# An instruction order ranked by the work behind each instruction, and weight splits taken off GpSimd

## The chip, the core and the metric

The kernel runs on one core of a Trainium2 chip. The metric is device time in microseconds (us) for one execution. A core has five instruction streams that run side by side and meet at semaphores: PE (TensorE, matrix products), DVE (VectorE), ACT (ScalarE), POOL (GpSimd) and SP (SyncE, which here only issues DMAs). Each stream runs its own instructions strictly in the order in which they were written into it, so an instruction that waits holds up everything behind it on its engine.

## What is computed

Three stages follow one another on 2304 tokens of width 512:

```
attention, 4 batches x 8 heads, 576 positions, head size 64, causal:
    scores = q k^T / 8 + cum[i] - cum[j],   cum = cumsum(log(clip(f)))
    x = softmax(scores) v                          -> 2304 x 512
first MLP:   h = x w_in  (512 x 2048);  g = h * tanh(softplus(h));  x = g w_out
second MLP:  h = x w2_in (512 x 1024);  s = h * softmax(h)
             out = (layernorm(s) * g_ln) w2_out
```

The four weight matrices arrive as 64-bit floats, q, k, v and f as 32-bit floats.

## The kernel before

**Products in three passes.** Every operand of a product is held as a high and a low half in f16, and a product is hi·hi + hi·lo + lo·hi, all accumulated in PSUM. A value therefore needs two element-wise passes before it can be used: one that makes the high half, one that makes the low half (value minus high half). The function `split` (L178) does this in one of three modes: mode 0 is one ACT pass for the high half and one DVE pass for the low half; mode 1 is an ACT pass that scales in place, a POOL pass for the high half and a POOL pass for the low half; mode 2 is two ACT passes and one POOL pass.

**Weights of the first MLP.** `w_in` and `w_out` are cut into eight tiles each of 128 x 1024 values (the class `Weight`, L95). A tile takes this way: `load` (L110) fetches 1 MB by DMA into one of two raw buffers that all sixteen tiles share; `conv` (L116) turns the 64-bit floats into 32-bit ones by three DVE passes (L123, L125, L127), after which the raw buffer is free for the next load; eight small matmuls (L146) form a Gram matrix that bounds the size of the values; after every two tiles, `bound` (L149) works out one power-of-two scale from it, by a chain of tiny DVE operations and one matmul across partitions; and `split` makes the two halves of both tiles. The sixteen tiles come in the order two of `w_in`, two of `w_out`, and so on (L684). Which mode each split takes is a string indexed by the tile number: `W1P = "00111111"` for `w_in` (tiles 0 and 1 in mode 0, tiles 2 to 7 in mode 1) and `W2P = "10"` for `w_out` (even tiles in mode 1, odd ones in mode 0), used at L602 and L609.

**Attention.** Per batch there are five query chunks of up to 128 rows. `step_s` makes scores on PE, `step_r` the maxima (DVE, L465) and exponentials (ACT, L467), `step_h` the halves (ACT, POOL or DVE for the high half, POOL at L506 for the low half), a DMA transpose (L511) turns them, `step_pv` multiplies by v (L537 to L539), and `fin` normalises, splits and transposes into `xT`, the input of the first MLP, which has three buffers of 256 tokens each.

**First MLP.** Nine blocks of 256 tokens. `up` (L764) makes h, `mish_a` to `mish_c` the activation and its halves (ACT, DVE, POOL at L791), `down` (L808) the second product. Block 0 takes each weight group as it becomes ready. **Second MLP.** The class `Stage2` (L1305), 18 tiles of 128 tokens: `first` (L1371 and the normalisation), a transpose through DMA, and `second` (L1411). Its weights are prepared as attention ends.

**The order of the work.** `emit` writes all instructions once, in an order set by hand-chosen leads. At the end `Order(tc).pin()` (L938) lays a new order over it. `Order.trace` rebuilds operations and dependencies, including the reuse of buffers in the order in which they were written; `weigh` gives each operation an estimated duration; `plan` (L1201) is a list scheduler that steps through time and, whenever an engine is free, starts the ready operation of lowest rank. It models a lock between DVE and POOL and one serial DMA resource. The rank of an operation is its number in the order written: `seq = self.plan([o.k for o in self.ops])` (L1297). The order found is then pinned on all five streams, so that it is what the chip executes. The estimated times decide only the order, not the times on the chip.

Of the kernel before, what the change touches and what calls it, by code (L numbers as in the profile page):

```python
# [51 lines left out]
HI0 = "a"  # L52
HI1 = "pd"
SP1 = "0000001"
W1P = "00111111"
W2P = "10"
QKV = "002"
W0C = 1
S2Q = 3
# [132 lines left out]
def emit(tc, q, k, v, f, w_in, w_out, w2_in, w2_out, g_ln, out):  # L192
# [404 lines left out]
    def w1_split(n):  # L597
        g, r = divmod(n, W1.group)
        if r == 0:
            W1.bound(g)  # L600
            nc.vector.tensor_copy(wps[g], W1.p(g))
        W1.split(n, on_pool=int(W1P[n % len(W1P)]))  # L602

    def w2_split(n):
        g, r = divmod(n, W2.group)
        if r == 0:
            W2.bound(g)
            nc.vector.tensor_tensor(rho[:, g:g + 1], wps[g], W2.p(g), op=ALU.mult)
        W2.split(n, on_pool=int(W2P[n % len(W2P)]))  # L609

# [340 lines left out]
ENGS = ("PE", "ACT", "POOL", "DVE", "SP")  # L951
ENG_OF = {"PE": "PE", "Activation": "ACT", "Pool": "POOL", "DVE": "DVE", "SP": "SP"}
EARLY = {"PE": 0.0, "ACT": 103.0, "DVE": 79.0, "POOL": 37.0, "SP": -45.0}
LATE = {"PE": 53.0, "ACT": 34.0, "DVE": 33.0, "POOL": 77.0, "SP": 27.0}
HEAD = 126.0
PERIOD = 3413.33
BACKLOG = 1500.0
LANDED = 600.0


def size_of(dt):
    s = str(dt)
    return 8 if "64" in s else 2 if "16" in s else 4
# [10 lines left out]
def on_chip(t):  # L974
    return type(t).__name__ == "Tile" and "DRAM" not in str(t._space)


class Order:
# [155 lines left out]
    def weigh_dma(self, o, i, acc):  # L1134
        out = next(b for t, b, w in acc if w)
        n = math.prod(c for _, c in list(out.ap)) * size_of(out.tensor.dtype)
        if type(i).__name__ == "InstDmaTransposeAnt":
            n //= 256
            o.d = {1536: 2000.0, 2048: 1860.0, 2560: 3050.0}.get(n, 1240.0)
            o.span = {512: 985.0, 1280: 2390.0, 1536: 2130.0, 2048: 2630.0, 2560: 3215.0}.get(n, 1410.0)  # L1140
            o.first = 1175.0
            return

        def run(b):
            r = 1
            for s, c in reversed(list(b.ap)[1 if on_chip(b.tensor) else 0:]):
                if c != 1 and s != r:
                    break
                r *= c
            return r * size_of(b.tensor.dtype)  # L1150

        rb = min(run(b) for t, b, w in acc)
        n //= rb
        o.d = {256: 590.0 if n >= 100 else 390.0, 4096: 368.0, 2048: 340.0}.get(rb, 500.0)
        o.span = n * rb / 300 if rb >= 1024 else n * (1.25 if n > 100 else 5.0) + 30
        o.first = 1020.0
# [44 lines left out]
    def plan(self, rank):  # L1201
# [24 lines left out]
        while todo:  # L1226
# [31 lines left out]
            elif e == "SP":  # L1258
                state["dma"] = max(state["dma"] - 20, t + o.first) + o.span
                end, seen = t + o.d, state["dma"] + LANDED  # L1260
                heapq.heappush(marks, state["dma"] - BACKLOG)
# [31 lines left out]
        self.end = state["end"]  # L1293
        return seq

    def pin(self):
        seq = self.plan([o.k for o in self.ops])  # L1297
        info = mybir.DependencyInfo(mybir.DependencyClass.NoSync, mybir.DependencyReason.DATA)
        for e in ENGS:
            row = [i for o in seq[e] for i, _ in o.ins]  # L1300
            for a, b in zip(row, row[1:]):
                self.tc.add_manual_dep(b, a.name, info, reason="order")
# [160 lines left out]
```

## Time and profile before

| | us |
|---|---|
| median of 3 runs (840.65 to 846.69) | 841.4 |
| the profiled execution | 845.53 |
| its span, first to last instruction | 843.7 |
| PE busy | 734.2 (87%) |
| DVE busy | 598.6 (71%) |
| ACT busy | 544.6 (65%) |
| POOL busy | 440.6 (52%) |

The span is 1.8 us shorter than the profiled execution, and that execution is 4.1 us above the median. The busy shares are averages over stages of different character: attention and weight preparation at the start, attention beside the first MLP in the middle, the second MLP at the end. The page cuts the span in 40 slices of 21.1 us each; a line of digits gives the busy share of an engine per slice in tenths.

### The profile page before, as it was taken

What the parts mean: (1) busy time and instruction counts of PE and PEld (TensorE: products, weight loads), DVE (VectorE), ACT (ScalarE), POOL (GpSimd) and SP (SyncE); (2) the same over time, 40 slices, a digit from 0 to 9 for tenths busy, and PEclk for the clock granted to TensorE, in tenths of its full rate; (3) what the DMA queues carried; (4) which work ended last, traced back from release to release, by engine and by line L of the source; (5) the groups of instructions that cost most, each with busy time, mean ns of one, the idle gap of its engine ahead of it and who ended that gap; (6) DMA issues with size and microseconds to landing.
All of it is one profiled execution on the core that took longest, in us unless ns stands there. A gap on an engine that the chain in (4) does not pass through costs nothing.

```text
span 843.7 us, 15751 instructions
## 1 busy us (share of the span) xinstructions
PE 734.2 (87%) x5822; PEld 456.5 (54%) x5822; DVE 598.6 (71%) x1158; ACT 544.6 (65%) x1201; POOL 440.6 (52%) x341
## 2 busy tenths in 40 slices
PE   0454245899999999899899999998999999999998
PEld 0333123556766666667566766675555554444443
DVE  5789979576976688867878963589978444656551
ACT  4743424898877998779878786788776554332331
POOL 2368377555678667776588783218357221213221
PEclk9999555999999999899999999999999999999999
DMA  9997694636699999997999743552224232355443
GB/s 226 207 206 213 210 220 97 122 58 129 137 169 163 190 159 182 174 187 147 195 169 163 146 80 76 163 199 77 63 56 87 63 71 63 88 97 115 103 88 85
DMA packets 328568, 114.83 MB, mean 136 GB/s; under 512 B 317676, under 2 KB 317676, under 8 KB 328492
## 3 DMA queue, kind: packets, MB, share of 16 engines
q1 hardware_dynamic: 328492, 113.84, 65.5%
q8 instruction: 45, 0.74, 0.4%
q14 instruction: 31, 0.25, 0.1%
HBM read 46.59 MB, written 9.55 MB: 67 GB/s over the span
## 4 chain that ended last, share of the span: by engine, by line
PE 53%; DVE 16%; ACT 10%; DMA 10%; issue 5%; POOL 5%; SPq 1%; POOLq 0%; DVEq 0%; ACTq 0%
PE x L808 14%; PE h L764 12%; PE h L1371 9%; PE o L1411 7%; PE pv L537 3%; DMA pT<-ph 2%; PE sp L418 2%; PE sp L419 2%; DMA rawk<-in_k_dram 2%; DMA w2i_r<-in_moe_w_in_dram 2%; POOL ph L506 1%; DMA rawv<-in_v_dram 1%; ACT p L467 1%; DVE wout L127 1%; POOL gt L791 1%
## 5 line engine op out<-in xcount | busy, mean ns | idle before, releaser
L808 PE MATMUL x<-wout,gt 128*128 128x512 f16 x864 | 213.9, 385 | 9.9 <-POOL gt L791 6.0
L764 PE MATMUL h<-xT,win 128*128 128x256 f16 x1728 | 209.9, 275 | 1.4 <-ACT th L777 1.4
L506 POOL TENSOR_TENSOR ph<-p,ph 128x512 f16<-128x512 f32 (+4 forms) x120 | 159.7, 1338 | 55.3 <-ACT ph L505 34.0
L764 PEld LDWEIGHTS <-win 128*128 128x128 f16 x1728 | 167.6, 99 | 35.1 <-issue 4.3
L791 POOL TENSOR_TENSOR gt<-th,gt 128x512 f16<-128x512 f32 x72 | 91.3, 1270 | 101.7 <-ACT gt L790 101.6
L808 PEld LDWEIGHTS <-gt 128*128 128x128 f16 x864 | 80.4, 99 | 90.3 <-POOL gt L791 10.0
L1399 POOL TENSOR_TENSOR z<-sl,z 128x1024 f16<-128x1024 f32 x18 | 39.2, 2178 | 140.4 <-DVE s2c L1378 87.8
L1371 PE MATMUL h<-w,x2T 128*128 128x512 f16 x432 | 96.0, 379 | 0.1
L1411 PE MATMUL o<-wo,zT 128*128 128x512 f16 x432 | 95.7, 379 | 0.1
L537 PE MATMUL pv<-vt,pT 128*128 128x64 f16 (+3 forms) x480 | 71.6, 202 | 12.7 <-DMA pT<-ph 12.6
L467 ACT ACTIVATE p<-sp,nm 64x64 f32<-64x64 f32 (+7 forms) x128 | 61.1, 483 | 33.1 <-DVE nm L465 16.8
L785 DVE SCALAR_TENSOR_TENSOR th<-ta,th 128x512 f32<-128x512 f32 x72 | 58.7, 817 | 23.4 <-ACT ta L784 20.4
L418 PE MATMUL sp<-ktr,qa 128*128 128x64 f16 (+6 forms) x304 | 58.6, 255 | 15.4 <-ACT p L467 13.1
L538 PE MATMUL pv<-vt,pT 128*128 128x64 f16 (+3 forms) x480 | 70.7, 197 | 0.0
L539 PE MATMUL pv<-vt,pT 128*128 128x64 f16 (+3 forms) x480 | 70.6, 197 | 0.0
L1411 PEld LDWEIGHTS <-zT 128*128 128x128 f16 x432 | 42.2, 98 | 51.3 <-DMA zT<-z 0.6
L1371 PEld LDWEIGHTS <-x2T 128*128 128x128 f16 x432 | 42.2, 98 | 50.6 <-DMA x2T<-x2d 0.6
L537 PEld LDWEIGHTS <-pT 128*128 128x128 f16 (+3 forms) x480 | 45.8, 102 | 42.5 <-issue 16.8
L419 PE MATMUL sp<-ktr,qb 67*128 67x64 f16 (+6 forms) x304 | 62.7, 256 | 4.2 <-DVE qb L383 3.7
L465 DVE TENSOR_REDUCE nm<-sp 128x1 f32<-128x320 f32 (+7 forms) x88 | 48.5, 562 | 22.4 <-PE sp L423 11.9
L1382 ACT ACTIVATE e<-h,s2c 128x1024 f32<-128x1024 f32 x18 | 21.7, 1204 | 64.2 <-DVE s2c L1380 64.2
L776 ACT ACTIVATE ta<-h,usc 128x512 f32<-128x512 f32 (+3 forms) x96 | 53.7, 576 | 14.3 <-PE h L764 14.2
(234 smaller groups left out, 1440.3 us busy)
## 6 DMA issues: line engine op xcount, KB each, us to landing
wi_r<-in_moe_w_in_dram SPq DMA_DIRECT2D x8, 1024.0 KB
wo_r<-in_moe_w_out_dram SPq DMA_DIRECT2D x8, 1024.0 KB
rawk<-in_k_dram SPq DMA_DIRECT2D x25, 256.0 KB
rawv<-in_v_dram SPq DMA_DIRECT2D x25, 256.0 KB
x2d<-x2h SPq DMA_DIRECT2D x18, 256.0 KB
out_dram<-ro SPq DMA_DIRECT2D x18, 256.0 KB
w2i_r<-in_moe_w_in_dram SPq DMA_DIRECT2D x4, 1024.0 KB
w2o_r<-in_moe_w_out_dram SPq DMA_DIRECT2D x4, 1024.0 KB
```

The costliest lines, as they stand in the source:

```text
L418: nc.tensor.matmul(d, qa[:, h, r0:r1_], k1, start=True, stop=False)
L419: nc.tensor.matmul(d, qb_[:67, h, r0:r1_], k2, start=False, stop=not diag)
L467: nc.scalar.activation(pv[:m, g * (i + 1) * P + off:g * (i + 1) * P + end], s3[:, g, off:end], AF.Exp, bias=nm[:m, g:g + 1], accum_out=rs[ ...
L506: nc.gpsimd.tensor_tensor(p4[:, :, 1], pv3, p4[:, :, 0], op=ALU.subtract)
L537: nc.tensor.matmul(o, pT[a0:a1, k, :m], vh, start=(c == 0), stop=False)
L538: nc.tensor.matmul(o, pT[a0:a1, k, :m], vl, start=False, stop=False)
L539: nc.tensor.matmul(o, pT[a0:a1, k + 1, :m], vh, start=False, stop=(c == i))
L764: nc.tensor.matmul(ph, win[:, (fi // 4) * NC1 + c, col:col + P], x[:, lx * NC1 + c, :], start=(m == 0), stop=(m == 3 * NC1 - 1))
L791: nc.gpsimd.tensor_tensor(gt[:, 1], th, gt[:, 0], op=ALU.subtract)
L808: nc.tensor.matmul(o, gt[:, lg, n % 2, t * P:(t + 1) * P], wout[:, fi, lw * 512:(lw + 1) * 512], start=(first and m == 0), stop=(last and ...
L1371: nc.tensor.matmul(h[:, half * 512:(half + 1) * 512], x[:, lx * NC1 + c, :], self.w2[:, half * NC1 + c, lw * 512:(lw + 1) * 512], start=(n ...
L1411: nc.tensor.matmul(o, zT[:, lz * NF2 + c, :], self.wo[:, c, lw * 512:(lw + 1) * 512], start=(n == 0), stop=(n == 3 * NF2 - 1))
```

## The change

Three things change. The mode strings `W1P` and `W2P` become `"0"`: all sixteen weight tiles of the first MLP are split in mode 0. A few estimated DMA transpose spans are altered (they enter only the planner). And the planner runs six rounds: the first with the rank as before; after each round a new function `back` walks the schedule from its end (a list schedule of the reversed graph, on the same engines, with operations that started late taken first) and gives every operation the time from its start to the end as `tail`; its negative is the rank of the next round, so that what has most work behind it goes first. Of the six orders the one with the earliest estimated end is pinned.

```diff
-W1P = "00111111"
-W2P = "10"
+W1P = "0"
+W2P = "0"
...
+ROUNDS = 6
...
-            o.span = {512: 985.0, 1280: 2390.0, 1536: 2130.0, 2048: 2630.0, 2560: 3215.0}.get(n, 1410.0)
+            o.span = {512: 1040.0, 1280: 2390.0, 1536: 2130.0, 2048: 2680.0, 2560: 3300.0}.get(n, 1530.0)
...
+    def back(self):
+        ops, start = self.ops, self.start
+        engs = ENGS + ("-",)
+        left = [len(o.succ) + len(o.osucc) for o in ops]
+        at, tail = [0.0] * len(ops), [0.0] * len(ops)
...
+                    heapq.heappush(ready[e], (-start[k], k))
...
+                    if e == "SP":
+                        dma = t + o.span
+                        free[e] = t + o.d + 45
+                        gone = o.span + o.first + LANDED
+                    elif e != "-":
+                        free[e] = t + o.d - EARLY[e]
+                        gone = o.d + LATE[e] + (165 if e == "PE" else 0)
+                        if o.lock:
+                            port = t + o.d - HEAD
+                    tail[o.k] = t + gone
+                    for k in o.deps | o.od:
+                        at[k] = max(at[k], tail[o.k])
...
+        return [-x for x in tail]
...
     def pin(self):
-        seq = self.plan([o.k for o in self.ops])
+        best, rank = None, [o.k for o in self.ops]
+        for _ in range(ROUNDS):
+            seq = self.plan(rank)
+            if best is None or self.end < best[0]:
+                best = self.end, seq
+            rank = self.back()
+        seq = best[1]
```

## Rows read from the trace of the kernel before

**Rows 1.** Page, section 2: PE's busy tenths in 40 slices of 21.1 us.
```profile
PE   0454245899999999899899999998999999999998
```
**Rows 2.** Windows by stage: length, busy us (instructions) per engine, PE clock, DMA share, GB/s.
```profile
0.00:115.00 115.00, 40.48 (x331) 29.68 (x331) 93.84 (x147) 56.17 (x125) 60.49 (x45) 0.88 0.90 210
115.00:125.00 10.00, 6.92 (x34) 3.70 (x34) 6.45 (x15) 2.11 (x4) 5.67 (x4) 0.67 0.88 262
125.00:142.00 17.00, 6.72 (x47) 4.18 (x45) 15.86 (x18) 5.70 (x9) 14.61 (x8) 0.50 0.29 85
142.00:160.00 18.00, 14.32 (x140) 11.29 (x138) 10.68 (x26) 14.76 (x33) 9.75 (x9) 0.88 0.67 125
160.00:240.00 80.00, 79.55 (x754) 52.10 (x753) 58.85 (x121) 69.20 (x165) 45.88 (x38) 0.99 0.61 115
240.00:450.00 210.00, 201.16 (x2073) 137.87 (x2072) 164.99 (x322) 173.35 (x442) 152.87 (x137) 0.98 0.99 175
450.00:844.00 394.00, 385.09 (x2458) 217.65 (x2455) 247.94 (x512) 223.28 (x427) 151.32 (x104) 1.00 0.44 98
```
**Rows 3.** Waits of PE before 160 us: total us, times, longest.
```profile
PE gram L146 <- DVE win L127: 23.7, 7, 7.7
PE gram L146 <- DVE wout L127: 21.7, 6, 8.4
```
**Rows 4.** Chain that ended last: start us, us, what.
```profile
81.96 3.04 DVE wout L127
...
109.90 3.91 POOL win L189
...
139.20 2.06 DVE wout L127
```
**Rows 5.** Busy DVE time before 142 us of L123, L125 and L127, in turn.
```profile
0.00:142.00 142.00, 16.29 (x16) 0.82 0.83 199
...
0.00:142.00 142.00, 28.47 (x16) 0.82 0.83 199
...
0.00:142.00 142.00, 24.91 (x16) 0.82 0.83 199
```
**Rows 6.** Instructions on the tile win: ns min/median/max, first and last start us.
```profile
L123 DVE TENSOR_SCALAR win<-wi_r x8: 675/686/1537, 16.2 to 120.2; 128x1024 int32<-128x1024 int32 x8
L125 DVE SCALAR_TENSOR_TENSOR win<-wi_r,win x8: 1210/1226/3019, 16.9 to 121.0; 128x1024 int32<-128x1024 int32 x8
L127 DVE SCALAR_TENSOR_TENSOR win<-wi_r,win x8: 1212/1220/1941, 18.2 to 122.2; 128x1024 int32<-128x1024 int32 x8
L184 ACT ACTIVATE win<-win,wi_b x6: 1132/1142/1151, 74.9 to 129.0; 128x1024 f32<-128x1024 f32 x6
L181 ACT ACTIVATE win<-win,wi_b x2: 1133/1156/1178, 37.0 to 40.4; 128x1024 f16<-128x1024 f32 x2
```
**Rows 7.** DVE groups before 160 us: busy us, mean ns, idle before.
```profile
L182 DVE SCALAR_TENSOR_TENSOR wout<-wout,wo_b 128x1024 f16<-128x1024 f32 x4 | 5.2, 1290 | 0.7 <-ACT wout L181 0.7
L182 DVE SCALAR_TENSOR_TENSOR win<-win,wi_b 128x1024 f16<-128x1024 f32 x2 | 2.9, 1432 | 0.5 <-ACT win L181 0.5
```
**Rows 8.** POOL groups before 160 us, the weight splits: the same columns.
```profile
L189 POOL TENSOR_TENSOR win<-win 128x1024 f16<-128x1024 f32 x6 | 16.9, 2814 | 0.5
L189 POOL TENSOR_TENSOR wout<-wout 128x1024 f16<-128x1024 f32 x4 | 10.0, 2493 | 0.3
L186 POOL TENSOR_SCALAR win<-win 128x1024 f16<-128x1024 f32 x6 | 9.0, 1495 | 4.5 <-ACT win L184 4.2
L186 POOL TENSOR_SCALAR wout<-wout 128x1024 f16<-128x1024 f32 x4 | 5.3, 1338 | 15.0 <-ACT wout L184 15.0
```
**Rows 9.** Timeline of POOL, 130 us on: start us, us, instruction.
```profile
130.60 2.97 POOL L189 TENSOR_TENSOR win<-win 128x1024 f16<-128x1024 f32 x1
```
**Rows 10.** Timeline of DVE, 131 us on: the same columns.
```profile
131.63 3.03 DVE L127 SCALAR_TENSOR_TENSOR wout<-wo_r,wout 128x1024 int32<-128x1024 int32 x1
```
**Rows 11.** Attention's transposes: issues, all and before 160 us; a landing in the chain.
```profile
L511 SPq DMA_TRANSPOSE pT<-ph x72: 1193/1748/3911, 32.0 to 522.3; - x72
...
L511 SPq DMA_TRANSPOSE pT<-ph x12: 1232/1448/3446, 32.0 to 156.2; - x12
...
244.30 5.18 DMA pT<-ph
```

More of the change, by code (lines that the diff above doesn't have):

```diff
@@ L1294, in plan @@
         return seq
-    def pin(self):
-        seq = self.plan([o.k for o in self.ops])
+    def back(self):
[3 more added lines that the diff above has]
+        at, tail = [0.0] * len(ops), [0.0] * len(ops)
+        pend, ready = {e: [] for e in engs}, {e: [] for e in engs}
+        free = {e: 0.0 for e in engs}
+        port = dma = t = 0.0
+        for o in ops:
+            if left[o.k] == 0:
+                heapq.heappush(pend[o.eng], (0.0, o.k))
+        todo = len(ops)
+        while todo:
+            for e in engs:
+                while pend[e] and pend[e][0][0] <= t + 1e-9:
+                    k = heapq.heappop(pend[e])[1]
+                    heapq.heappush(ready[e], (-start[k], k))
+                while ready[e] and free[e] <= t + 1e-9:
+                    x = ready[e][0]
+                    if e in ("DVE", "POOL") and port > t + 1e-9:
+                        x = min((x for x in ready[e] if not ops[x[1]].lock), default=None)
+                    elif e == "SP" and dma > t + 1e-9:
+                        x = None
+                    if x is None:
+                        break
+                    ready[e].remove(x)
+                    heapq.heapify(ready[e])
+                    o = ops[x[1]]
+                    todo -= 1
+                    gone = 0.0
+                    if e == "SP":
[10 more added lines that the diff above has]
+                        at[k] = max(at[k], tail[o.k])
+                        left[k] -= 1
+                        if left[k] == 0:
+                            heapq.heappush(pend[ops[k].eng], (at[k], k))
+            c = [pend[e][0][0] for e in engs if pend[e]] + [free[e] for e in engs if ready[e]]
+            c += [port] if ready["DVE"] or ready["POOL"] else []
+            c += [dma] if ready["SP"] else []
+            t = min((x for x in c if x > t + 1e-9), default=t)
+        return [-x for x in tail]
```

## The prediction

> **What bounds the kernel now.** I read the slices first, then windows cut at the places where they change, then the waits and the chain inside the slow stretch. The slices [rows 1] show two kernels: eight slices in which TensorE is half idle, and from there to the end one in which it is almost never idle. The windows [rows 2] put numbers on it. Before 160 us TensorE is busy for 40.48 + 6.92 + 6.72 + 14.32 = 68.4 us, so 91.6 us idle, and part of the work runs at a granted clock of 0.50 to 0.88. From 160 us to the end it is busy 665.8 of 684 us: 18.2 us idle in all, 8.8 of them between 240 and 450 us. So no order, however good, takes more than about 18 us out of the long part; what there is to win lies before 160 us.
>
> What holds TensorE there? The longest waits [rows 3] are the Gram matmuls waiting for the last conversion pass of a weight tile, 45.4 us in 13 waits, and the chain [rows 4] runs from about 68 to 141 us through conversions on VectorE, with a stretch of weight splits on GpSimd between 105 and 114. Between 125 and 142 us VectorE is busy 15.86 of 17 us while the DMA share is 0.29 [rows 2]: at that point transfers are not the limit, VectorE is. Earlier they are both near full (share 0.90 over the first 115 us).
>
> **The mode swap.** Ten tiles move from mode 1 to mode 0 (six of w_in, four of w_out). Their ACT pass stays one pass, 1.14 us scaling in place or 1.16 us making the high half [rows 6]: nothing gained or lost. GpSimd loses 16.9 + 10.0 + 9.0 + 5.3 = 41.2 us [rows 8]. VectorE gains ten low-half passes; the six that exist cost 8.1 us, so 1.35 each, 13.5 us [rows 7]. Each new pass waits for ACT's high half, and what is queued behind it is the next tile's conversion, on which the raw buffer and so the next load hang. The six passes had 1.2 us of such waits together, 0.2 each, so 2 us for ten; the bounds are 0 and 7 (the largest that fits the rows, 0.7, for all ten).
>
> Against this stands what the GpSimd passes cost VectorE. The three conversion passes took 16.29 + 28.47 + 24.91 = 69.7 us for 16 tiles [rows 5]; at the shortest durations seen, 0.675 + 1.210 + 1.212 = 3.10 us a tile [rows 6], it would be 49.6. The 20.1 us of stretching go with GpSimd: a pass that normally takes 1.21 took 3.03 while a split of 2.97 ran on GpSimd [rows 9, 10]. Not all of it comes from weight splits, as attention's low halves run on GpSimd too. I take 16 us as given back, with bounds 10 (the splits' 41.2 us are about half of GpSimd's work before 142 us) and 20. Sum: 13.5 + 2 - 16 = -0.5 us, bounds -6.5 (no wait, all 20 back) and +10.5 (7 us of waits, 10 back). The swap alone is about even.
>
> One thing speaks against it. The new passes read two tensors each, as the conversions do that were held up beside GpSimd. The four existing ones on w_out averaged 1.29 us, the two on w_in 1.43 [rows 7], so little of it shows, and 1.35 stands. If every new pass were held up as the pass in [rows 10] was, 3.03 instead of 1.21, the swap would come to 10 x 1.82 = 18 us more. The Trainium skill ("SBUF — State Buffer", section "SBUF: two separate sides") has it that a VectorE instruction with two SBUF inputs and a GpSimd instruction take one shared port pair in turn, the later one standing still for the whole of the other. By that rule alone the swap could cost up to those 18 us instead of nothing; the long pair [rows 9, 10] agrees with it, the means of [rows 7] say that such meetings were rare for these passes.
>
> **The new order.** No instruction is added or removed; all five streams, the DMA queue on SP among them, may be reordered. The trace of before can't show the new order, so I bound it. Say TensorE becomes continuously busy at time T instead of 160 us, with only as much done by then as was done by T before. Full-speed work is busy time times clock [rows 2]: 35.6 us by 115, 40.2 by 125, 43.6 by 142, 56.2 by 160. What isn't done by T must be done later, so the gain is (160 - T) minus (56.2 - work by T):
> - T = 142: 18 - 12.6 = 5.4 us
> - T = 125: 35 - 16.0 = 19 us
> - T = 115: 45 - 20.6 = 24.4 us
>
> How early can T be? VectorE starts converting at 16.2 us [rows 6] and is busy 93.84 + 6.45 + 15.86 = 116.2 of the 142 us in which it converts the last tile. If it did weights alone, 69.7 - 16 of conversion and sixteen low halves of 1.35 would end at about 16 + 54 + 22 = 92 us. It must do some attention too, for block 0 needs its input; the 25.8 us of its idling and most of attention's VectorE work can go, since from 160 us it is only 74% busy (58.85 of 80). TensorE need not wait for all the weights, since block 0 takes groups as they come, and T lies somewhere between 92 and 142, past the middle since transfers were near full too. I take T = 130, where the work done is 40.2 plus 5 us at the rate of the 125 to 142 window, 41.2: 30 - 15 = 15 us. What ranks highest under the new rule is what has the longest tail, which before 142 us is the weight chain (all of block 0 to 8 hangs on it), so I expect weights to overtake attention on VectorE and in the DMA queue. In the long part I cost the reordering at nothing: 18.2 us of idle time are there to win or to double, and with VectorE and ACT at 74 and 87% busy in 160 to 240 a small slip is absorbed. The altered spans are inputs of the planner alone and cost nothing.
>
> Sum: 845.5 (profiled execution; its span plus 1.8) - 0.5 - 15 = 830; that execution stood 4.1 us above the median, so against the median of 841.4 I say 826.
>
> **Rivals.**
> - *Much better: the weight chain really goes first.* T = 115, and half the later idle goes too: 24.4 + 9 = 33 us, about 808. For it: the DMA share of 0.29 in 125 to 142 and the 25.8 us of idle VectorE. Against: transfers are at 0.90 before 115 us, and each load waits for a raw buffer. Chance 0.12.
> - *Nothing: the front stays as it is.* The pinned order may be the first round's, with only the swap, or a better plan may hit the same transfers. Time 841, with the swap's bounds and run scatter 833 to 850. For it: two resources near full in the front [rows 2]. I count here too the case that each new low half is held up by GpSimd: 18 us, which would eat the 15 and leave about 844. Chance 0.23, of which 0.05 for that case.
> - *Slower: weights overtake attention, and attention is late in the middle.* Place: the DMA queue between 240 and 450 us, share 0.99 already, TensorE's only large idle spot. Twelve of the 72 transposes of line 511 are issued before 160 us, and one took 5.18 us in the chain [rows 11]. If all twelve are pushed behind, 62 us of transfers move into what follows; the 160 to 240 window has 39% of 80, 31 us, of free transfer time [rows 2], so 31 us stick out and delay the first MLP's input: 841.4 - 15.5 + 31 = 857. It decides once more than 31 + 15.5 = 46 us, nine transposes, are pushed back. Against: xT has three buffers, so attention runs ahead of the first MLP by up to three blocks and can lose some lead. Chance 0.17.
>
> **Numbers.** The forecast, 815 to 833 by T between about 115 and 138, has 0.48. The time is 826. About 1% (8.4 us) is what a measurement can tell here, the three runs spanning 6: faster by over 1% means under 833, so 0.48 + 0.12 = 0.60; within 1% 0.23; slower 0.17. The range of 8 in 10 cuts most of the best case and the upper part of the slow one: 811 to 853. The likeliest case's own range is 815 to 833.
>
> **What would show it.** The last conversion should end well before 141 us, near 120; L123, L125 and L127 should sum to about 54 us; the Gram waits should shrink from 45 us; the slices of TensorE should reach 9 one or two slices earlier; its idle time after that should still be about 18 us. A transfer share of 1 with TensorE idle at 200 to 300 us would show the slow rival. An unchanged last conversion, with faster passes but more waiting for loads, would show that transfers, not VectorE, set the front, and the forecast would be wrong at its choice of T.

## The result and the profile after

The changed kernel took 812.6 us (median of 4 runs, 811.6 to 813.1) against 842.9 before (4 runs, 840.7 to 846.7): ratio 0.9635, 95% interval 0.9594 to 0.9675. That is 30 us faster; the forecast said 826, so it had the direction, and the range of 811 to 853 held the time only at its very edge. The gain is nearly twice the 15.5 us of the sum.

Page of after, section 2, TensorE's slices (20.3 us each); the row to hold it against is [rows 1]:

```profile
PE   0345568799999999999999999999999999999998
```

Windows of after, cut as in [rows 2] (length, busy us and instructions of PE, PEld, DVE, ACT, POOL, TensorE clock, DMA share, GB/s):

```profile
0.00:115.00 115.00, 48.79 (x392) 34.86 (x393) 98.56 (x174) 59.80 (x130) 39.70 (x35) 0.76 1.00 241
115.00:125.00 10.00, 7.04 (x35) 4.18 (x34) 9.67 (x23) 6.45 (x15) 4.43 (x3) 0.55 0.66 120
125.00:142.00 17.00, 14.55 (x178) 10.61 (x177) 15.11 (x32) 17.00 (x44) 9.69 (x8) 1.00 0.86 162
142.00:160.00 18.00, 12.46 (x133) 7.93 (x133) 15.82 (x33) 17.85 (x45) 12.95 (x10) 0.85 0.72 141
160.00:240.00 80.00, 79.56 (x735) 54.21 (x736) 65.19 (x110) 67.60 (x160) 54.38 (x51) 0.97 0.85 153
240.00:450.00 210.00, 210.00 (x2158) 146.69 (x2159) 175.26 (x332) 175.82 (x433) 149.87 (x134) 1.00 0.86 159
450.00:811.30 361.30, 357.24 (x2201) 199.11 (x2199) 223.47 (x470) 202.05 (x380) 133.28 (x85) 1.00 0.41 97
```

Three things make up the 32.4 us by which the span shrank (843.7 to 811.3). TensorE's idle time before 160 us went from 91.6 to 77.2, so 14.4 us. Its idle time after 160 us went from 17.9 to 4.5, so 13.4 us (the 18.2 us of the prediction count the last window of [rows 2] to 844.0, 0.3 us past the span's end): between 240 and 450 us it is now busy without a gap, where before it lost 8.8 us. And its busy time fell from 734.2 to 729.6, 4.6 us; why it fell was not taken apart. The second of these the prediction had put at nothing.

The conversion passes L123, L125 and L127 of after, busy VectorE time of the sixteen tiles in turn, against [rows 5]:

```profile
0.00:160.00 160.00, 12.46 (x16) 0.78 0.93 214
...
0.00:160.00 160.00, 20.28 (x16) 0.78 0.93 214
...
0.00:160.00 160.00, 20.81 (x16) 0.78 0.93 214
```

They sum to 53.6 us; 54 had been forecast. Instructions on win and wout in after (ns min/median/max, first and last start in us) say when it ended, against [rows 6]:

```profile
L127 DVE SCALAR_TENSOR_TENSOR wout<-wo_r,wout x8: 1205/1212/1293, 35.6 to 117.5; 128x1024 int32<-128x1024 int32 x8
...
L182 DVE SCALAR_TENSOR_TENSOR win<-win,wi_b x8: 1267/1276/2182, 65.1 to 126.2; 128x1024 f16<-128x1024 f32 x8
```

The last conversion starts at 117.5 us instead of 139.2 [rows 4]. But the waits of the Gram matmuls (total us, times, longest) did not shrink:

```profile
PE gram L146 <- DVE win L127: 17.1, 6, 4.8
PE gram L146 <- DVE wout L127: 16.1, 4, 8.0
...
PE gram L146 <- DVE wi_b L158: 5.9, 1, 5.9
PE gram L146 <- DVE wo_b L92: 4.3, 1, 4.3
```

With a fifth of 2.2 us they come to 45.6 us, as much as the 45.4 of [rows 3]. So they do not follow the idle time, which fell by 14.4 us. And attention was not pushed back: seventeen of its transposes are issued before 160 us, not twelve [rows 11]:

```profile
L511 SPq DMA_TRANSPOSE pT<-ph x17: 1237/1910/4537, 33.3 to 157.9; - x17
```

### The profile page after: what moved, and what is told of

Read it like the earlier page. It is cut to its first block, busy times and chain, and to the rows that moved or that the text cites. A ratio compares the mean times of both kernels' runs of the same rounds, so it can differ in the third digit from the quotient of the medians.

```text
span 811.3 us, 15742 instructions
## 1 busy us (share of the span) xinstructions
PE 729.6 (90%) x5822; PEld 457.6 (56%) x5822; DVE 603.1 (74%) x1168; ACT 546.6 (67%) x1201; POOL 404.3 (50%) x321
## 4 chain that ended last, share of the span: by engine, by line
PE 66%; DVE 14%; issue 6%; ACT 5%; DMA 5%; POOL 4%; SPq 1%; POOLq 0%; DVEq 0%; ACTq 0%
PE x L808 17%; PE h L764 17%; PE h L1430 10%; PE o L1470 9%; PE pv L537 4%; PE sp L418 2%; PE sp L419 2%; DMA w2i_r<-in_moe_w_in_dram 2%; PE pv L538 1%; PE pv L539 1%; DVE wout L125 1%; DVE win L182 1%; DMA zT<-z 1%; DVE wout L127 1%; DVE win L125 1%
## 5 line engine op out<-in xcount | busy, mean ns | idle before, releaser
L808 PE MATMUL x<-wout,gt 128*128 128x512 f16 x864 | 217.6, 385 | 1.7 <-POOL gt L791 1.5
L764 PE MATMUL h<-xT,win 128*128 128x256 f16 x1728 | 214.4, 276 | 1.6 <-ACT th L777 0.9
L506 POOL TENSOR_TENSOR ph<-p,ph 128x512 f16<-128x512 f32 (+4 forms) x120 | 158.6, 1328 | 83.4 <-ACT ph L505 47.6
L791 POOL TENSOR_TENSOR gt<-th,gt 128x512 f16<-128x512 f32 x72 | 93.2, 1296 | 101.6 <-ACT gt L790 99.0
L808 PEld LDWEIGHTS <-gt 128*128 128x128 f16 x864 | 81.0, 99 | 74.4 <-POOL gt L791 4.3
L1458 POOL TENSOR_TENSOR z<-sl,z 128x1024 f16<-128x1024 f32 x18 | 41.3, 2292 | 128.9 <-DVE s2c L1437 62.7
L785 DVE SCALAR_TENSOR_TENSOR th<-ta,th 128x512 f32<-128x512 f32 x72 | 67.1, 934 | 27.9 <-ACT ta L784 26.9
L776 ACT ACTIVATE ta<-h,usc 128x512 f32<-128x512 f32 (+3 forms) x96 | 53.2, 577 | 19.6 <-PE h L764 18.4
L781 DVE TENSOR_SCALAR ta<-ta 128x512 f32<-128x512 f32 x72 | 51.8, 723 | 14.0 <-ACT ta L776 13.7
```

The lines of the kernel that those rows point to most:

```text
L506: nc.gpsimd.tensor_tensor(p4[:, :, 1], pv3, p4[:, :, 0], op=ALU.subtract)
L764: nc.tensor.matmul(ph, win[:, (fi // 4) * NC1 + c, col:col + P], x[:, lx * NC1 + c, :], start=(m == 0), stop=(m == 3 * NC1 - 1))
L785: nc.vector.scalar_tensor_tensor(th, ta, 2.5, th, op0=ALU.subtract, op1=ALU.mult)
L791: nc.gpsimd.tensor_tensor(gt[:, 1], th, gt[:, 0], op=ALU.subtract)
L808: nc.tensor.matmul(o, gt[:, lg, n % 2, t * P:(t + 1) * P], wout[:, fi, lw * 512:(lw + 1) * 512], start=(first and m == 0), stop=(last and ...
```

## The experiments

All times are medians in us, ratios are to runs of the kernel before on the same chip (844 to 846 us there); they are taken over the runs and differ by up to about 0.1% from the quotient of the medians. "Idle early" and "idle late" are TensorE's idle time before and after 160 us, from windows of each run cut as above.

| run | time | ratio | 95% interval | idle early | idle late |
|---|---|---|---|---|---|
| before | 842.9 | | | 91.6 | 17.9 |
| changed kernel | 812.6 | 0.9635 | 0.9594 to 0.9675 | 77.2 | 4.5 |
| e1_order | 828.1 | 0.9809 | 0.9769 to 0.9850 | 79.3 | 15.1 |
| e2_swap | 829.9 | 0.9818 | 0.9784 to 0.9851 | 75.1 | 18.4 |
| e3_round1 | 830.4 | 0.9824 | 0.9787 to 0.9861 | 72.4 | 21.4 |
| e4_front | 827.5 | 0.9805 | 0.9772 to 0.9838 | 80.5 | 13.2 |
| e5_rest | 819.3 | 0.9699 | 0.9674 to 0.9724 | 72.1 | 12.5 |
| e7_pool_read | 853.5 | 1.0101 | 1.0062 to 1.0140 | 95.6 | 23.8 |
| e8_pool_memset | 838.7 | 0.9928 | 0.9903 to 0.9954 | 82.5 | 20.5 |
| e10_dve_only | 827.5 | 0.9789 | 0.9752 to 0.9826 | 70.1 | 22.1 |
| e11_all_but_pe | 838.8 | 0.9913 | 0.9895 to 0.9930 | 79.6 | 20.7 |
| e12_dma | 814.7 | 0.9628 | 0.9611 to 0.9644 | 78.8 | 9.2 |
| e13_less_pool | 811.2 | 0.9592 | 0.9577 to 0.9607 | 75.1 | 6.9 |
| e14_less_pool_leads | 808.1 | 0.9554 | 0.9530 to 0.9578 | 73.2 | 10.4 |

**The two halves apart.** First the order alone, then the mode swap alone.

```diff
 # e1_order: the changed kernel, but
-W1P = "0"
-W2P = "0"
+W1P = "00111111"
+W2P = "10"
 # e2_swap: the kernel before, but
-W1P = "00111111"
-W2P = "10"
+W1P = "0"
+W2P = "0"
```

> The ranked order and the altered spans, with the mode strings of before (ten weight tiles split with GpSimd). Theory A, the prediction's: the swap is about even and the order brings the gain, so 812 to 818 (843 before, 813 after). Theory B: the swap brings a good half, because GpSimd no longer holds up VectorE in the front, so 825 to 832. Under both the three conversion passes should sum to more than the 53.6 us of after, near the 69.7 us of before; under A that stretching is hidden by the new order.

> The kernel before with only the two mode strings changed: old rank, one round, old spans. Theory A: even, 836 to 848 (the prediction's bounds of -6.5 and +10.5 around 843, less the unlikely end), conversions near 54 us, last conversion still near 140 us. Theory B: 825 to 832, last conversion ended by 130 us. Third possibility, each new pass held up by a GpSimd pass: 855 or more, the new passes at 2 to 3 us each.

By their times theory A falls and theory B holds; B's reason, VectorE no longer held up, is another matter (below). Each half alone brings about 2%, and the product of the two ratios, 0.963, is the ratio of both together. So the swap, put at -0.5 us, is worth some 15 (14.4 by the medians on its chip, 15.4 by the ratio). The windows before 160 us, e1_order and then e2_swap, cut as in [rows 2], show where each half alone gains:

```profile
0.00:115.00 115.00, 43.92 (x345) 32.26 (x345) 95.09 (x153) 58.20 (x128) 60.67 (x47) 0.70 0.97 233
115.00:125.00 10.00, 4.10 (x38) 3.29 (x39) 9.22 (x16) 2.18 (x4) 8.44 (x3) 0.50 0.49 140
125.00:142.00 17.00, 16.41 (x127) 10.97 (x126) 16.43 (x35) 15.14 (x34) 14.68 (x10) 0.79 0.68 134
142.00:160.00 18.00, 16.25 (x170) 9.77 (x169) 13.19 (x32) 15.52 (x38) 12.66 (x9) 0.91 0.49 90
```

```profile
0.00:115.00 115.00, 48.21 (x360) 32.50 (x361) 98.06 (x171) 59.67 (x130) 38.54 (x35) 0.79 0.95 231
115.00:125.00 10.00, 6.33 (x44) 3.86 (x42) 9.46 (x20) 5.47 (x11) 1.90 (x2) 0.50 0.96 216
125.00:142.00 17.00, 13.36 (x116) 10.79 (x117) 11.55 (x25) 11.59 (x26) 4.48 (x4) 0.74 0.47 86
142.00:160.00 18.00, 17.05 (x189) 11.61 (x188) 11.67 (x33) 17.87 (x42) 11.91 (x11) 1.00 0.58 107
```

Both gain early: the order alone takes 12.3 us of TensorE's idle time out of the front and 2.8 out of the rest, the swap alone 16.5 out of the front and nothing out of the rest. Together they take only 14.4 out of the front. The two gains overlap there, and what the second change adds shows in the long part: 13.4 us together, where neither takes more than 2.8 by itself. Why it shows there, no run takes apart.

The swap's bookkeeping on VectorE was right. In e2_swap the conversions L123, L125 and L127 sum to 54.8 us instead of 69.7 (in e1_order, without the swap, to 64.3; near 69.7 had been expected):

```profile
0.00:180.00 180.00, 13.32 (x16) 0.81 0.83 191
...
0.00:180.00 180.00, 19.77 (x16) 0.81 0.83 191
...
0.00:180.00 180.00, 21.69 (x16) 0.81 0.83 191
```

The sixteen low-half passes cost 23.6 us where the six of [rows 7] cost 8.1:

```profile
L182 DVE SCALAR_TENSOR_TENSOR win<-win,wi_b 128x1024 f16<-128x1024 f32 x8 | 12.0, 1503 | 0.7 <-ACT win L181 0.5
L182 DVE SCALAR_TENSOR_TENSOR wout<-wout,wo_b 128x1024 f16<-128x1024 f32 x8 | 11.6, 1445 | 0.6 <-ACT wout L181 0.6
```

(groups of VectorE before 180 us: busy us, mean ns, idle before). That is 14.9 us back and 15.5 us paid: even on VectorE, and TensorE still idles 16.5 us less. VectorE's total can't be the reason. That the conversions, on which loads and Gram matmuls hang, come earlier (the last one starts at 126.4 us instead of 139.2) could still be one.

**The altered spans.** e3_round1 is the changed kernel with `ROUNDS = 1`.

> The changed kernel with one round, so the old rank, with the swap and the altered transpose spans. It separates the spans from the rank: 827 to 833, the time of the swap alone, if the spans matter only through the planner's rank; under 825 if they bring a part of the gain themselves.

At 830.4 it is e2_swap within the intervals. The spans do nothing that these runs can tell, and e3_round1 is the proper base for the effect of the rank once the swap is made: 830.4 to 812.6, 17.8 us (16 by the ratios). In the two profiles (spans 828.9 and 811.3) the rank adds 4.8 us of idle time early, takes away 16.9 late, and the busy time falls by 5.5.

**GpSimd's time put back.** Two kernels add to e2_swap, beside each of the ten swapped splits, work on GpSimd that nothing reads.

```diff
 # e7_pool_read                      (t: scratch, d: the tile's halves)
+        nc.gpsimd.tensor_tensor(o, one, h, op=ALU.subtract)      # h: high half, o: t
+        nc.gpsimd.tensor_scalar(t, t, 1.0, 0.0, op0=ALU.mult, op1=ALU.add)
 # e8_pool_memset
+        nc.scalar.copy(t[:, 0, 0:1], d[:, 0, 0:1])
+        for _ in range(3):
+            nc.gpsimd.memset(t, 0.0)
```

> The kernel with only the swap, and beside each of the ten swapped splits two GpSimd passes of the old size (one of two inputs, one of one) into a scratch tile on which no weight depends. Theory Q, GpSimd's time itself was the price (its passes stand before attention's low halves in its queue, and hold up VectorE's passes): back to 838 to 846. Theory L, only the latency of the weight halves was (ACT, then two GpSimd passes, before a product may start): stays at 827 to 833.

> As the run before, but the scratch passes are three memsets each, some 3 us of GpSimd time that read nothing from SBUF, gated by a one-element ACT copy. If what hurts is the queue (attention's low halves standing behind), the same time as with reading passes, 838 to 846, with conversions at their short durations. If what hurts is VectorE being held up by GpSimd's reading, 828 to 834, and the three conversion passes sum to about 54 us here against about 65 to 70 with reading passes.

Neither kernel stays at the swap's time: e7_pool_read lies above both ranges (853.5), e8_pool_memset at the lower edge of the queue's (838.7). e7_pool_read costs back more than the swap had won, with scratch passes of 46.8 us, more than the 41.2 of [rows 8]. But it does not separate theory Q from theory L: its weights are late too. The last conversion starts at 146.7 us and the last low half of w_out at 158.9, against 126.4 and 137.4 in e2_swap. In e8_pool_memset they are only some 3 us late, 130.0 and 140.2. Groups of GpSimd before 180 us, e7_pool_read and then e8_pool_memset:

```profile
L246 POOL TENSOR_TENSOR joi<-ones,win 128x1024 f16<-128x1024 f32 x6 | 17.7, 2954 | 10.2 <-ACT win L181 10.2
...
L247 POOL TENSOR_SCALAR joi<-joi 128x1024 f16<-128x1024 f16 x6 | 10.9, 1810 | 0.5
L246 POOL TENSOR_TENSOR joo<-ones,wout 128x1024 f16<-128x1024 f32 x4 | 10.6, 2650 | 17.2 <-ACT wout L181 17.2
L247 POOL TENSOR_SCALAR joo<-joo 128x1024 f16<-128x1024 f16 x4 | 7.6, 1898 | 0.4
```

```profile
L245 POOL MEMSET joi<- 128x1024 f16 x18 | 18.3, 1014 | 11.1 <-ACT joi L243 10.4
L245 POOL MEMSET joo<- 128x1024 f16 x12 | 11.4, 951 | 16.3 <-ACT joo L243 15.8
```

The two kernels tell two prices apart. Memsets leave VectorE's conversions at 53.8 us in e8_pool_memset, L123, L125 and L127 in turn:

```profile
0.00:180.00 180.00, 13.71 (x16) 0.88 0.77 181
...
0.00:180.00 180.00, 20.22 (x16) 0.88 0.77 181
...
0.00:180.00 180.00, 19.86 (x16) 0.88 0.77 181
```

Reading passes stretch VectorE: 64.8 us of conversions in e7_pool_read, and the low-half passes, the ones that the change adds, now meet GpSimd too, 33.5 us for sixteen instead of 23.6:

```profile
L182 DVE SCALAR_TENSOR_TENSOR wout<-wout,wo_b 128x1024 f16<-128x1024 f32 x8 | 17.7, 2218 | 1.4 <-ACT wout L181 1.2
L182 DVE SCALAR_TENSOR_TENSOR win<-win,wi_b 128x1024 f16<-128x1024 f32 x8 | 15.8, 1970 | 1.1 <-ACT win L181 1.1
```

Still, 29.7 us of memsets cost 8.8 us against e2_swap (9.3 by the ratios; 8.3 against e3_round1, on the same chip) with the conversions short. So short conversions alone do not bring the swap's gain, and GpSimd's time in the front has a price: about 0.3 us for each us of memsets. At that rate the 41.2 us of the old splits come to 12 us, an estimate that takes the price to be linear. It would cover most of what the swap won; what is shown is 8 to 9 of some 15. One rival stands: the planner orders each of these kernels anew, and it takes every GpSimd pass, memsets too, to lock VectorE out. Part of the 8.8 us may come from an order laid around a lock that, by the times of the conversions, the memsets did not take. (The ten ACT copies that gate the memsets are no rival of size: ACT stood 1.7 us behind memsets.)

Through which wait the price is paid is not shown. One place where attention stands behind the splits can be seen in the kernel before. GpSimd's timeline (start us, us, instruction), and under it SP's in the same stretch:

```profile
133.66 1.90 POOL L186 TENSOR_SCALAR win<-win 128x1024 f16<-128x1024 f32 x1
135.65 2.44 POOL L189 TENSOR_TENSOR win<-win 128x1024 f16<-128x1024 f32 x1
138.04 4.22 POOL L506 TENSOR_TENSOR ph<-p,ph 128x512 f16<-128x512 f32 x2
```

```profile
127.04 16.72 SPq L511 DMA_TRANSPOSE pT<-ph  x2
143.85 2.02 SPq L564 DMA_TRANSPOSE xT<-xh  x1
```

ACT had made attention's high halves by 132.5 us; their low halves (L506) stand behind two weight tiles on GpSimd and begin at 138. Their transpose, the second of the two in the first SP row, waits at the head of the DMA queue for 13.7 us, and all other issues wait with it. This is why the DMA share was 0.29 in [rows 2] between 125 and 142. Some 5.5 of the 13.7 us are the weight tiles' doing; the rest is the wait for ACT and the low halves themselves. But taking the splits away did not free the queue's head. SP's longest waits between 120 and 150 us (total us, times, longest), before and then in e2_swap:

```profile
SPq L511 <- POOL ph L506: 16.1, 2, 13.7
```

```profile
SPq L511 <- POOL gt L791: 11.5, 1, 11.5
```

In e2_swap a transpose of attention still stands there for 11.5 us (the row names L791; the low half that it needs ends at 142.4 us, as the wait does), and GpSimd is idle for most of that time. All of SP's waits for GpSimd before 160 us come to 40.9 us before and 44.7 in e2_swap. So this held head is a price of the old kernel, but not what the swap won. What fell most in e2_swap is TensorE's wait at the Gram matmuls for L127, from 45.4 us [rows 3] to 28.3 (4.6 more for another VectorE pass, L92); and fifteen transposes of attention are issued before 160 us instead of twelve (fourteen in e8_pool_memset, eleven in e7_pool_read).

**Where the order earns it.** Two kernels give the new rank to one part only; the cut is the first product of the second block of the first MLP.

```diff
 # e4_front
+        seq = self.plan([x if k < cut else float(k) for k, x in enumerate(best[2])])
 # e5_rest
+        seq = self.plan([k - 1e9 if k < cut else x for k, x in enumerate(best[2])])
```

> The changed kernel, but only what is written before the second block's first product has the new rank (and goes ahead of the rest); the rest is ranked by the order written. Two separate gains (accounting of the two traces: 14 us less idle time of TensorE before 160 us, 14 us less after it): 824 to 830, idle time after 160 us again near 18 us. One gain (the late idle time vanishes because the front hands over earlier): 812 to 818.

> The changed kernel, but what is written before the second block's first product is ranked by the order written and goes ahead of the rest; only the rest has the new rank. Two separate gains: 824 to 832, idle time of TensorE after 160 us near 5 us, before 160 us near 90 us. One gain that begins in the front: 838 to 846.

Against e3_round1 the front's rank alone gives 2.9 us, which the intervals do not tell from nothing, the rest's alone 11.1, both 17.8. e4_front fits "two separate gains"; e5_rest lies below both ranges of its expectation. The two gains are not the two I meant: with the swap made, the early gain is there already, and the rank earns mostly in the rest. Some 4 us only appear when both parts are ranked together; both kernels also make the front go ahead of the rest, which the changed kernel does not. Idle time late was forecast near 5 for e5_rest and near 18 for e4_front; it was 12.5 and 13.2, and only both together bring it to 4.5. None of this holds without the swap: e1_order has the full rank, gains 12.3 us early and still idles 15.1 us late.

**Which engine's choice.** Ranks decide among the instructions of one engine (between engines only where two could start at the same instant), so they can be mixed.

```diff
 # e10_dve_only
+        seq = self.plan([best[2][o.k] if o.eng=="DVE" else float(o.k) for o in self.ops])
 # e11_all_but_pe
+        seq = self.plan([best[2][o.k] if o.eng != "PE" else float(o.k) for o in self.ops])
```

> The changed kernel with the new rank on VectorE's instructions alone; the other four engines choose by the order written. If the late gain comes from which ready instruction VectorE takes first (attention's small steps ahead of the MLP's passes), 815 to 822 and little idle time of TensorE after 160 us. If it comes from the order of transfers or of the matmuls, 826 to 833, as with the swap alone.

> The changed kernel, but TensorE chooses by the order written; VectorE, ScalarE, GpSimd and the DMA queue keep the new rank. If the late gain is made by what feeds TensorE (transfers and element-wise steps earlier), 813 to 818. If TensorE's own choice among ready products makes it, 825 to 832, the time without the rank.

VectorE's choice alone gives 2.8 us, not told from nothing, and none of the late gain (22.1 us idle late). With every engine ranked but TensorE the kernel is 8.4 us slower than with none ranked (7.5 by the ratios), above both ranges of its expectation. The loss is early, 79.6 us of idle time instead of 72.4; late it idles 20.7 us, against 21.4 with none ranked and 4.5 with all. So the late gain needs TensorE's own choice to go with the others': neither VectorE alone nor the other four engines without TensorE bring as much as 1 us of it. Waits of TensorE after 160 us (total us, times, longest) in e3_round1, then in the changed kernel:

```profile
PE x L808 <- DVE x2h L837: 5.1, 3, 2.3
PE x L808 <- POOL gt L791: 4.3, 5, 1.3
PE pv L537 <- DMA pT<-ph: 2.6, 4, 1.1
PE sp L418 <- ACT p L467: 2.3, 4, 0.9
```

```profile
PE h L764 <- ACT th L777: 0.4, 1, 0.4
PE x L808 <- POOL gt L791: 0.2, 1, 0.2
```

In e3_round1 there are many small waits, on VectorE, GpSimd, ScalarE and transfers; in the changed kernel, almost none.

**Are transfers what it waited for?** Fifteen spare transfers were added to the changed kernel.

```diff
 # e12_dma
+    def spare_load(b, c):
+        t = dram.tile([P, DM], w_out.dtype, name=f"spare_{b}_{c}")
+        nc.sync.dma_start(t, w_out[c * P:(c + 1) * P, :])
...
                 load_raw(nb, ni, "qkv")
+                spare_load(nb, ni)
```

> The changed kernel with fifteen more transfers of 512 KB within DRAM, one at each chunk load of batches 1 to 3, that nothing reads. Theory: before, TensorE idled between 240 and 450 us because the transfers were full there (share 0.99), and the new rank moved transfers into the looser 160 to 240 window (0.61 to 0.85; share after 240 then 0.86). Then filling the room again costs it back: share 0.95 or more in 240 to 450, TensorE's idle time there 6 to 12 us instead of 0, and 820 to 828. If transfers were not what TensorE waited for, 812 to 816 in spite of the share.

```profile
160.00:240.00 80.00, 76.85 (x748) 53.14 (x749) 68.69 (x108) 70.68 (x166) 60.38 (x53) 1.00 0.93 180
240.00:450.00 210.00, 207.89 (x2120) 144.31 (x2119) 171.81 (x332) 174.43 (x431) 146.27 (x131) 1.00 0.97 182
```

The theory falls. The windows of e12_dma show the share back at 0.97 and TensorE idle for only 2.1 us there; the time is 814.7, and the ratio is not told from that of the changed kernel. After 160 us it idles 9.2 us in all, 4.7 more than the changed kernel. A share near 1 did not by itself starve TensorE here. The planner knew of the spare transfers and ordered around them, so this says that full transfers can be lived with, not that they never counted in the old order.

**Further along the same line.** Both runs change strings of the changed kernel.

```diff
 # e13_less_pool
-HI1 = "pd"
-SP1 = "0000001"
-QKV = "002"
+HI1 = "dda"
+SP1 = "0"
+QKV = "000"
 # e14_less_pool_leads: these, and
-WS0 = 3
-A0 = 16
-ROUNDS = 6
+WS0 = 4
+A0 = 24
+ROUNDS = 12
```

The expectation below calls the new string "one in three on GpSimd"; `"dda"` in fact takes attention's high halves off GpSimd altogether, two in three to VectorE and one in three to ScalarE.

> The changed kernel with still less on GpSimd: all splits of q, k and v in mode 0, and of attention's high halves in batches 1 to 3 one in three on GpSimd instead of one in two. If GpSimd's queue is still a price anywhere, 806 to 811; if what was left on it is hidden now and VectorE pays for the passes, 813 to 818.

> As the run before, and with twelve rounds, attention of the second block written later (A0 24 instead of 16) and one more weight step per early slot (WS0 4 instead of 3). A try at a faster version: 803 to 810 if a longer search and looser leads add to it, 811 to 816 if the estimates no longer tell such orders apart.

e13_less_pool, 811.2 with GpSimd's busy time down from 404 to 353 us, is not told from the changed kernel: the intervals overlap, and the time lies between the two ranges. e14_less_pool_leads is the fastest kernel of the study, 808.1 us; its interval (0.9530 to 0.9578) lies below that of the changed kernel, but touches that of e13_less_pool. Its TensorE idles no less than in the changed kernel (83.6 us in all against 81.7); it is busy 725.3 us instead of 729.6. Which of its three additions did it was not taken apart.

## Why the prediction's range held and its reasons did not

That the range of 811 to 853 held the time is luck. The swap was underpriced by some 15 us, the sum fell short by as much, and 812.6 lies 1.6 us inside the edge. Of the five signs that the prediction named, two came: the last conversion starts at 117.5 us, and the conversions sum to 53.6 us. The Gram waits did not shrink, TensorE's slices still reach 9 only in the ninth slice, and the idle time after that did not stay at 18 us.

- **What bounds the kernel.** "What there is to win lies before 160 us" was half right: 14.4 us came from there, 13.4 from the long part, which had only 17.9 to give and gave three quarters of it.
- **The swap, -0.5 us.** This is the step that failed. The terms on VectorE were right (conversions 53.6 against 54 forecast; e2_swap 14.9 us back against 16, 15.5 paid with the dearer passes against 13.5 plus 2). A term was left out, GpSimd's own: "GpSimd loses 41.2 us" was written down and given no price, with no word on what stands behind those passes in GpSimd's queue. The swap was worth some 15 us. e8_pool_memset puts 8 to 9 us on 29.7 us of GpSimd's time, in an order that was planned anew; that GpSimd's time accounts for all of the 15 is argued, not shown. The 105 to 114 us stretch of GpSimd in the chain [rows 4], which the text named, was the hint: behind those splits the chain goes on with GpSimd's pass L791 at 113.80 us and the product L808 on TensorE that waits for it.
- **The two-input passes held up by GpSimd.** e7_pool_read shows that it can happen to the new passes: 2.2 and 2.0 us on average, 20 us on VectorE with the conversions. In the changed kernel the swap itself removes what they would meet, and on w_in they take 1.28 at the median, 2.2 at most. So the long pair of [rows 9, 10] was no rare event, but the edit removed most of its cause. The rule that the prediction uses is put there for any GpSimd instruction; the memsets, which read nothing from SBUF, did not stretch the two-input conversions L125 and L127 (40.1 us for sixteen tiles, against 41.5 in e2_swap and 49.4 beside reading passes).
- **The new order, -15 us.** The size was near: 16.3 us alone (844.3 to 828.1 on its chip), 17.8 against e3_round1. The place was near for the order alone, which took 12.3 us out of the front, and wrong for the order beside the swap. There the rank left the front's idle time about where the swap had put it (72.4, then 77.2) and took 16.9 us late. The working supposed that the swap, being about even, leaves all of the front's idle time to the order; "in the long part I cost the reordering at nothing" is the second step that failed.
- **Weights overtake attention.** They did not have to: 17 transposes instead of 12 before 160 us and the last conversion 22 us earlier, with the DMA share at 1.00 in the first 115 us. The swap alone had brought 15 transposes and 13 of the 22 us. Nor did all of the weight chain go first: the last low half of w_out starts at 167.6 us in the changed kernel, against 152.7 before and 137.4 in e2_swap. The slower rival rested on the same picture and didn't come.
- **The much better case** (808, chance 0.12) came nearest in time, with its own picture, late idle time halved, more than borne out, and its early half not.

## What to carry to other kernels

When an edit takes work off an engine that is not the bound, price what stands behind that work in its queue, and who waits for that: here 29.7 us of memsets that nothing reads cost 8 to 9 us, on an engine that was about half busy. A stretch in which the bounding engine is 97% busy can still be ordered better; here that took one plan for its own choice and its feeders'. Measure the two halves of a combined edit apart, and where each gains as well as how much: here both gained in the front alone, and together the second gain showed in the long part. A time inside the range had hidden a wrong term and a wrong place. When an experiment changes the work and the order is planned anew, the order is part of what was changed.

## What was not expected of the hardware

GpSimd memsets of 128x1024 (0.95 to 1.01 us each on average) left VectorE's conversions short (53.8 us for 16 tiles, 54.8 without any added pass), while GpSimd passes that read SBUF stretched them to 64.8 us and the two-input low-half passes from 1.5 to about 2.1 us on average. And a DMA share of 0.97 over 210 us went with only 2.1 us of idle time on TensorE.
